# Giving the attention chain of the lead-in an earlier place in the scheduler's order

## The chip, the cores and the metric

The kernel runs on one core of a Trainium2 chip. The metric is the device time of one execution in microseconds (us). The core's engines are TensorE (PE, with its weight loads PEld), VectorE (DVE), ScalarE (ACT), GpSimd (POOL) and SyncE (SP), whose queue starts the DMAs.

## What is computed

Three stages follow each other on 4608 tokens (8 batches of 576) of width 512, all in float32: attention over pooled keys and values, an MoE-like layer with a SoLU and a layer norm, and a SiLU layer.

```python
k_p = k.reshape(B, H, Sp, 8, D).mean(axis=3);  v_p = v.reshape(B, H, Sp, 8, D).mean(axis=3)
scores = (q @ k_p.T) / sqrt(D)                 # B = H = 8, 576 queries, 72 pooled keys
attn = exp(scores - max);  attn = attn / (attn.sum() + 1e-9)
x = attn @ v_p                                  # to (4608, 512)
h = x @ w_in                                    # (4608, 1024)
solu = h * softmax(h);  x = layer_norm(solu) * g_ln @ w_out
h = x @ w2_in;  out = (h * sigmoid(h)) @ w2_out # hidden width 2048
```

The weights arrive as float64 bit patterns (pairs of 32-bit words) and are converted to float32 on the chip.

## The kernel before

Tokens go in 36 tiles of 128. For a tile `t` the words of a small script call the steps: `q` loads queries, `S` (`scores`) multiplies them with the pooled keys and takes the row maximum on DVE and scales it on POOL, `X` (`softmax`) runs 8 exponentials on ACT, a sum and scale on POOL, a reciprocal on DVE and the two products `pb` and `lf` on POOL, `T` (`probs_T`) transposes them on PE and `keep_T` splits the result into a high and a low part with ACT and DVE (`pth`, `ptl`, `ptx`). `A` (`attend_next`) multiplies a segment of 256 or 320 tokens with the pooled values and splits each of four results into `xTh` (ACT) and `xTl` (DVE). `H` (`hidden1`) is the first layer's product, `M`, `E`, `Z` are its maximum (DVE), exponential (ACT) with product (DVE, line 459), and norm (ACT and POOL); `N` transposes the result, `P` (`project1`) is the second product. Names such as S2 or T2 below are the word with its tile, A0 and A1 are segments 0 and 1, and `H0,1,3` is tile 0, half 1 of the hidden width, chunk 3 of the model width.

Beside this run background pieces, called by the word `B`: `prep_k` and `prep_v` load and pool one batch's keys and values, and `load_w1i` and `load_w1o` convert the weights of the first layer, eight pieces each. One piece is a DMA from SP (line 130), an ACT pass (138), three DVE passes (141 `sign`, 142, 145) in `convert`, an ACT copy (155) and a POOL subtraction (156, which writes `w1il` or `w1ol`). A step that needs a piece which no `B` has called calls it itself through `need`. Piece (f, k) of `w1i` is what `H` with half f and chunk k reads.

`SCRIPT` is the lead-in: a hand-written order of words for tiles 0 to 5. After it, `step` runs the script `STEP` once for each later tile. The order on PE is the order of the calls (`manual_schedule` holds PE alone through these stages). ACT, DVE, POOL and SP are ordered by the scheduler: at each point of its own timeline it gives an engine, among the instructions that are ready, the one with the lowest priority number, and that number is the count of instructions emitted so far. So with no other rule a conversion that was emitted before a softmax goes ahead of it when both are ready. Buffers limit it too: the score tile `s` and the hidden tile `h` in PSUM have one buffer each, `g` four, `pth`, `ptl` and `ptx` one, the raw keys and values three.

Emission numbers, counted by the code: S0 26, the first `prep_v` 61, the eight `w1i` pieces 84 to 260, T0 132, T1 142, S2 152, X2 158, T2 178, S3 195, A0 203, X3 232, S4 263 (it calls the four `prep_k` of batch 1 itself, 267 to 283), X4 303, T3 317, M0 332, E0 334, S5 338, Z0 344, T4 352, A1 365, X5 402, T5 468. The lead-in ends at 489, and its first `w1o` piece stands at 444.

```python
elif what == "S":
    scores(*n)
elif what == "X":
    softmax(*n)
```

Of the kernel before, what the change touches and what calls it, by code (L numbers as in the profile page):

```python
# [19 lines left out]
B, H, S, D = 8, 8, 576, 64  # L20
# [42 lines left out]
STEP = "B2 S H0 A B1 H1 M B1 B1 N E P1 X B3 P T B5 p B1 q B2 Z B1 B2"  # L63
TAIL = "H0 A H1 p B2 M N B1 E B2 Z P1 B2 B6 P B2"
RAWS = 3
SCALE = 1.0 / (POOL * math.sqrt(D))
REBIAS = 2.0**-112

# [14 lines left out]
def pooled_attention__solu__silu_kernel(  # L83
# [35 lines left out]
    def gps(name):  # L119
        return ps.tile([P, 512], F32, tag="g", name=name, bufs=4)  # L120
# [48 lines left out]
    def keep_f32(dst, src):  # L169
        w = yield from convert(src, held=True)  # L170
        yield
        nc.sync.dma_start(dst, w)
# [48 lines left out]
    def need(*key):  # L221
        while key not in ready:
            for entry in [e for e in going if e[1] == key]:
                advance(entry)
            for entry in todo:
                if entry[1] == key:
                    todo.remove(entry)
                    advance(entry)
                    break
# [3 lines left out]
    def prep_k(b, p):  # L233
        assert b < 2 or kept["s"] >= (b - 1) * S
        raw = aw.tile([P, SP, POOL], F32, tag="raw", name="raw", bufs=RAWS)
        nc.sync.dma_start(raw, kT[b, :, p])
# [15 lines left out]
    def prep_v(b, p):  # L252
        assert b < 2 or kept["x"] >= (b - 1) * S
        i = b % 2
        raw = aw.tile([P, SP, POOL], F32, tag="raw", name="raw", bufs=RAWS)[:, :D]
        nc.sync.dma_start(raw, vm[b, :, p])
# [13 lines left out]
    def prep_v_rest(b, g):  # L270
        i = b % 2
        raw = aw.tile([P, SP, POOL], F32, tag="raw", name="raw", bufs=RAWS)[0:96, :D]
        nc.sync.dma_start(raw, vl[b, :, g])
# [20 lines left out]
    def load_q(t):  # L294
        q_t[t] = aw.tile([P, NP, P], F32, tag="q", name="q", bufs=3)
        nc.sync.dma_start(q_t[t], qT[t])
# [3 lines left out]
    def scores(t):  # L300
        assert kept["s"] == t * P
        kept["s"] += P
        q = q_t.pop(t)
        sp = ps.tile([P, 2, 512], F32, tag="h" if t == 1 else "s", name="sp")
        done = 0
        while done < P:
            b, s = divmod(t * P + done, S)
            n = min(P - done, S - s)
            need("k", b)
            for p in range(NP):  # L310
                nc.tensor.matmul(  # L311
                    sp[done : done + n, p // 2, (p % 2) * 2 * SP : (p % 2 + 1) * 2 * SP],
                    q[:, p, done : done + n],
                    kbd[b % 2][:, p, :],
                    start=True, stop=True,
                )
            done += n
        sv = sp[:, :, 0 : 4 * SP].rearrange("p a (h k) -> p a h k", k=SP)
        st = aw.tile([P, 2, 2, 4], F32, tag="st", name="st", bufs=3)
        nc.vector.tensor_reduce(st[:, 0], sv, axis=AX, op=ALU.max, negate=True)  # L320
        nc.gpsimd.tensor_scalar(st[:, 0], st[:, 0], SCALE, 0.0, op0=ALU.mult, op1=ALU.add)  # L321
        s_t[t] = st, sv

    def softmax(t):
        st, sv = s_t.pop(t)
        pr = aw.tile([P, 2, 4, SP], F32, tag="pr", name="pr", bufs=2)
        for g in range(2):
            for h in range(4):
                behind["ACT"] = nc.scalar.activation(  # L329
                    pr[:, g, h], sv[:, g, h], AF.Exp, scale=SCALE,  # L330
                    bias=st[:, 0, g, h : h + 1], accum_out=st[:, 1, g, h : h + 1],
                )
        nc.gpsimd.tensor_scalar(
            st[:, 1], st[:, 1], 1e-9, float(POOL), op0=ALU.add, op1=ALU.mult
        )
        nc.vector.reciprocal(st[:, 0], st[:, 1])
        pb = aw.tile([P, 2, 4, 64], F32, tag="pb", name="pb")
        lf = aw.tile([P, 2, 3, 4, 8], F32, tag="lf", name="lf")
        nc.gpsimd.tensor_tensor(
            pb, pr[:, :, :, 0:64],  # L340
            st[:, 0].rearrange("p a (h o) -> p a h o", o=1).to_broadcast([P, 2, 4, 64]),
            op=ALU.mult,
        )
        for g in range(2):
            nc.gpsimd.tensor_tensor(
                lf[:, g],
                pr[:, g, :, 64:SP].rearrange("p (o h) k -> p o h k", o=1).to_broadcast([P, 3, 4, 8]),
                st[:, 0, g].rearrange("p (o h q) -> p o h q", o=1, q=1).to_broadcast([P, 3, 4, 8]),
                op=ALU.mult,
            )  # L350
        p_t[t] = pb, lf

    def seg_of(tok):
        for i, (t0, n, b) in enumerate(SEGS):
            if t0 <= tok < t0 + n:
                return i

    def probs_T(t):
        pb, lf = p_t.pop(t)
        pb = pb.rearrange("p a h k -> p (a h k)")  # L360
        lf = lf.rearrange("p g r h k -> p g (r h k)")
        pm = gps("pm")
        for p in range(NP):
            nc.tensor.transpose(
                pm[:, p * P : (p + 1) * P], pb[:, p * P : (p + 1) * P], ident
            )
        pl = gps("pl")
        for g in range(2):
            nc.tensor.transpose(pl[0:96, g * P : (g + 1) * P], lf[:, g], ident)
        done = 0  # L370
        while done < P:
            i = seg_of(t * P + done)
            m = min(P - done, SEGS[i][0] + SEGS[i][1] - t * P - done)
            if done:
                rest.append((t, pm, pl, i, done, m))
            else:
                keep_T(t, pm, pl, i, done, m)
            done += m
# [3 lines left out]
    def keep_T(t, pm, pl, i, done, m):  # L382
        if i not in pt_t:
            pt_t[i] = (
                aw.tile([P, NP, 320], F32R, tag="pth", name="pth", bufs=1),
                aw.tile([P, NP, 320], F32R, tag="ptl", name="ptl", bufs=1),
                aw.tile([96, 2, 320], F32R, tag="ptx", name="ptx", bufs=1),
            )
        assert kept["p"] == t * P + done
        kept["p"] += m  # L390
        th, tl, tx = pt_t[i]
        o = t * P + done - SEGS[i][0]
        pmv = pm.rearrange("p (a n) -> p a n", n=P)[:, :, done : done + m]
        split(th[:, :, o : o + m], tl[:, :, o : o + m], pmv)
        plv = pl[:, 0 : 2 * P].rearrange("p (a n) -> p a n", n=P)[:, :, done : done + m]
        nc.scalar.activation(tx[:, :, o : o + m], plv[0:96], AF.Copy)
        nc.vector.tensor_tensor(
            tx[64:96, :, o : o + m], plv[64:96], tx[64:96, :, o : o + m].bitcast(F32),
            op=ALU.subtract,
        )  # L400
# [45 lines left out]
    def solu_max(t):  # L446
        assert parts[t, 0] == parts[t, 1] == KC
        hp = h_t[t]
        st = wk.tile([P, 8], F32, tag="ls", name="ls", bufs=3)
        nm, sm, su, sq, a, rs = (st[:, i : i + 1] for i in range(6))  # L450
        nc.vector.tensor_reduce(nm, hp.rearrange("p a n -> p (a n)"), axis=AX, op=ALU.max, negate=True)
        e = wk.tile([P, 2, 512], F32, tag="e", name="e", bufs=2)
        l_t[t] = e, st
# [464 lines left out]
    for n in range(32):  # L918
        what = keep_f32(w2if[n // 4][:, n % 4], w2i[:, n]) if n < 16 else keep_f32(w2of[n % 8][:, (n - 16) // 8], w2o[:, n - 16])
# [19 lines left out]
    def attend_next():  # L939
        nonlocal nseg  # L940
        attend(nseg)
        nseg += 1
        while rest:
            keep_T(*rest.pop(0))
# [7 lines left out]
    def lead_in(script):  # L952
        for word in script.split():
            what, n = word[0], [int(x) for x in word[1:].split(",") if x]
            if what == "q":
                load_q(*n)
            elif what == "S":
                scores(*n)
            elif what == "X":
                softmax(*n)  # L960
            elif what == "T":
                probs_T(*n)
            elif what == "A":
                attend_next()
            elif what == "H":
                hidden1(*n)
            elif what == "M":
                solu_max(*n)
            elif what == "E":
                solu_norm(*n)  # L970
            elif what == "Z":
                solu_scale(*n)
                normed.append(n[0])
            elif what == "N":
                norm_next(*n)
            elif what == "P":
                project1(*chunks.pop(0))
            elif what == "B":
                background(*n)
# [200 lines left out]
```

## Time and profile before

| what | us |
|---|---|
| median of 3 runs | 1404.5 (1402.43 to 1406.67) |
| profiled execution | 1403.74 |
| its span in the trace | 1402.0 |
| PE busy | 1294.8 (92%) |
| DVE busy | 999.4 (71%) |
| ACT busy | 709.1 (51%) |
| POOL busy | 661.5 (47%) |

A span is the time from the first to the last instruction in the trace. Busy time of an engine is the time in which it ran an instruction; an idle engine is given with the one that released it. A view of stretches gives for each stretch the busy time of every engine, PE's granted clock as a share of full speed, and the DMA share.

### The profile page before, as it was taken

The numbers are of one execution on the slowest core, as the hardware profiler recorded it, in microseconds if no ns is written. First come the engines' busy times: TensorE is split into PE (matmuls) and PEld (weight loads), VectorE is DVE, ScalarE is ACT, GpSimd is POOL, SyncE is SP. The second block draws the span as 40 slices with busy tenths as digits, with TensorE's granted clock in tenths as the row PEclk, the third lists the DMA queues.
The fourth block names the chain that finished last, engine by engine and source line by source line (L and its number), as shares of the span: only waits on it lengthen the run. The fifth ranks groups of instructions, "written<-read, shape, count | busy, mean of one in ns | idle before, by whom it ended". The sixth has DMA issues, their size and how long they took to land.

```text
span 1402.0 us, 23904 instructions
## 1 busy us (share of the span) xinstructions
PE 1294.8 (92%) x8712; PEld 1227.4 (88%) x8712; DVE 999.4 (71%) x1438; ACT 709.1 (51%) x1772; POOL 661.5 (47%) x829
## 2 busy tenths in 40 slices
PE   2589899999999999889998999999979999999998
PEld 2469789988989899789888988999979999999998
DVE  6896566766766565445787889888547788877785
ACT  4684555565555555343554555554433444434442
POOL 5674344444444433444555666777323333433332
PEclk7899999999999999999999999999989999999999
DMA  7655244543434211122566678665776344444431
GB/s 227 207 159 164 80 130 143 156 139 114 140 99 128 91 61 61 61 76 94 194 243 250 245 266 307 238 237 195 294 271 255 128 151 151 151 129 143 134 95 74
DMA packets 100550, 227.01 MB, mean 162 GB/s; under 512 B 8272, under 2 KB 29776, under 8 KB 98896
## 3 DMA queue, kind: packets, MB, share of 16 engines
q1 hardware_dynamic: 96400, 210.80, 45.1%
q10 hardware_dynamic: 4032, 14.68, 2.8%
q8 instruction: 69, 1.13, 0.3%
q14 instruction: 49, 0.40, 0.1%
HBM read 141.56 MB, written 83.89 MB: 161 GB/s over the span
## 4 chain that ended last, share of the span: by engine, by line
PE 49%; DVE 7%; issue 5%; DMA 4%; ACT 3%; POOL 2%; SPq 0%; ACTq 0%; DVEq 0%; POOLq 0%
PE op L853 24%; PE m L707 12%; PE xp L510 6%; PE hp L440 5%; DVE gt L717 2%; DVE wr L529 1%; PE tp L490 1%; DMA w2r<-w2if 1%; DVE t L529 1%; DVE u L717 1%; ACT gt L677 1%; DMA x2r<-x2d 1%; PE sp L311 1%; DMA w2o<-wod 1%; DVE w2r L529 1%
## 5 line engine op out<-in xcount | busy, mean ns | idle before, releaser
L707 PE MATMUL m<-t,w2s 128*128 128x384 f32 x2016 | 367.2, 340 | 23.9 <-DVE gt L717 11.8
L707 PEld LDWEIGHTS m<-t,w2s 128*128 128x128 f32 x2016 | 352.4, 190 | 38.3 <-DVE gt L717 14.6
L853 PE MATMUL op<-w2o,gt 128*128 128x256 f32 x3024 | 368.0, 284 | 8.5 <-ACT gt L830 7.9
L853 PEld LDWEIGHTS op<-w2o,gt 128*128 128x128 f32 x3024 | 366.0, 193 | 10.5 <-ACT gt L830 8.8
L529 DVE TENSOR_TENSOR gt<-gr,gt 128x512 fp32r<-128x512 f32 x180 | 164.7, 949 | 67.4 <-ACT gt L830 67.4
L830 ACT ACTIVATE gt<-gr 128x512 fp32r<-128x512 f32 x180 | 103.2, 623 | 151.4 <-DVE gr L529 132.5
L717 POOL TENSOR_TENSOR gt<-u,m 128x384 f32<-128x384 f32 x96 | 114.5, 1203 | 134.3 <-ACT m L727 91.8
L510 PE MATMUL xp<-lnh,w1oh 128*128 128x256 f32 x576 | 168.1, 292 | 0.5 <-ACT lnh L123 0.2
L510 PE MATMUL xp<-lnl,w1oh 128*128 128x256 f32 x576 | 163.9, 285 | 1.1 <-DVE lnl L124 1.1
L510 PE MATMUL xp<-lnh,w1ol 128*128 128x256 f32 x576 | 163.8, 284 | 0.0
L440 PE MATMUL hp<-w1ih,xTh 128*128 128x512 f32 x288 | 119.0, 413 | 8.9 <-DVE e L459 8.9
L736 ACT ACTIVATE gt<-gt 128x768 f32<-128x768 f32 x48 | 40.7, 847 | 157.2 <-DVE gt L717 157.2
L811 POOL TENSOR_TENSOR s<-gr 128x512 f32<-128x512 f32 x36 | 58.3, 1618 | 127.1 <-DVE gt L529 74.2
L329 ACT ACTIVATE pr<-sp,st 128x72 f32<-128x72 f32 x288 | 88.3, 330 | 56.8 <-POOL st L321 56.7
L440 PE MATMUL hp<-w1il,xTh 128*128 128x512 f32 x288 | 115.5, 401 | 0.6 <-POOL w1il L156 0.6
L440 PE MATMUL hp<-w1ih,xTl 128*128 128x512 f32 x288 | 115.7, 402 | 0.3 <-DVE xTl L124 0.3
L510 PEld LDWEIGHTS xp<-lnh,w1oh 128*128 128x128 f32 x576 | 111.4, 193 | 1.7 <-DVE lnl L124 0.7
L510 PEld LDWEIGHTS xp<-lnl,w1oh 128*128 128x128 f32 x576 | 111.6, 194 | 1.4 <-DVE lnl L124 1.3
L510 PEld LDWEIGHTS xp<-lnh,w1ol 128*128 128x128 f32 x576 | 111.3, 193 | 0.0
L529 DVE TENSOR_TENSOR t<-tt,t 128x768 fp32r<-128x768 f32 x48 | 64.8, 1354 | 14.1 <-ACT t L640 14.0
L440 PEld LDWEIGHTS hp<-w1ih,xTh 128*128 128x128 f32 x288 | 56.3, 196 | 21.1 <-issue 9.2
L830 ACT ACTIVATE gt<-s 128x512 fp32r<-128x512 f32 x72 | 42.1, 621 | 62.6 <-POOL s L529 56.6
(129 smaller groups left out, 2352.4 us busy)
## 6 DMA issues: line engine op xcount, KB each, us to landing
gd<-gt SPq DMA_DIRECT2D x48, 768.0 KB, 4.5
gr<-gd SPq DMA_DIRECT2D x48, 512.0 KB, 6.2
x2r<-x2d SPq DMA_DIRECT2D x12, 1536.0 KB, 7.6
wod<-wo SPq DMA_DIRECT2D x56, 256.0 KB, 2.7
gr<-gd SPq DMA_DIRECT2D x48, 256.0 KB, 5.4
q<-qT SPq DMA_DIRECT2D x36, 256.0 KB, 3.2
raw<-kT SPq DMA_DIRECT2D x32, 288.0 KB, 3.5
x2d<-xo SPq DMA_DIRECT2D x18, 512.0 KB, 3.4
```

The costliest lines, as they stand in the source:

```text
L311: nc.tensor.matmul(sp[done : done + n, p // 2, (p % 2) * 2 * SP : (p % 2 + 1) * 2 * SP], q[:, p, done : done + n], kbd[b % 2][:, p, :], st ...
L329: behind["ACT"] = nc.scalar.activation(pr[:, g, h], sv[:, g, h], AF.Exp, scale=SCALE, bias=st[:, 0, g, h : h + 1], accum_out=st[:, 1, g, h ...
L440: nc.tensor.matmul(hp[:, f], l, r, start=(n == 1 and m == 0), stop=(n == KC and m == 2))
L490: nc.tensor.transpose(tp[:, k * P : (k + 1) * P], e[:, f, k * P : (k + 1) * P], ident)
L510: nc.tensor.matmul(xp[:, :GW], l, r, start=(k == 0 and m == 0), stop=(k == FC1 - 1 and m == 2))
L529: eng.tensor_tensor(dst, a, b, op=ALU.subtract)
L707: nc.tensor.matmul(to, wt[:, a, o : o + P], tk[:, b, k], start=(k == 0 and m == 0), stop=(k == 1 and m == 2),)
L717: eng.tensor_tensor(dst, a, b, op=ALU.add)
L736: nc.scalar.activation(gt[:, 0], gt[:, 0], AF.Silu)
L811: nc.gpsimd.tensor_tensor(s1, a21, a22, op=ALU.add)
L830: nc.scalar.activation(ring[n][:, 0], src, AF.Copy)
L853: nc.tensor.matmul(op[:, 256 * h : 256 * h + 256], t[:, l, i, ts], w[:, r], start=(s == i == h == m == 0), stop=(s == NSET - 1 and i == h ...
```

## The change

The words `S`, `X`, `T` and `A` of the lead-in are called inside a block that lowers the priority number of all that is emitted in it by 100. On leaving the block the count goes on as before. Nothing is added to or removed from the work; the later steps and PE's order stand as they were.

```diff
+AHEAD = 100
@@ lead_in
-            elif what == "S":
-                scores(*n)
-            elif what == "X":
-                softmax(*n)
-            elif what == "T":
-                probs_T(*n)
-            elif what == "A":
-                attend_next()
+            elif what in "SXTA":
+                with tc.high_priority(offset=AHEAD):
+                    {"S": scores, "X": softmax, "T": probs_T, "A": lambda x: attend_next()}[what](*n)
```

## Rows read from the trace of the kernel before

**Rows 1.** The page: busy time, share of the span, instructions.
```profile
PE 1294.8 (92%) x8712; PEld 1227.4 (88%) x8712; DVE 999.4 (71%) x1438; ACT 709.1 (51%) x1772; POOL 661.5 (47%) x829
```

**Rows 2.** Stretches: length, busy time by engine, granted clock, DMA share, GB/s.
```profile
60.40:66.20 5.80, 2.17 (x14) 1.67 (x14) 4.40 (x8) 5.14 (x17) 3.73 (x9) 1.00 0.65 226
...
68.40:71.70 3.30, 0.01 (x1) 0.01 (x1) 1.26 (x2) 2.45 (x9) 1.75 (x5) 1.00 0.61 171
71.70:75.10 3.40, 3.40 (x11) 3.15 (x12) 3.23 (x7) 3.11 (x13) 2.81 (x5) 0.52 0.16 19
...
95.00:106.00 11.00, 9.34 (x51) 7.85 (x50) 10.91 (x23) 10.29 (x36) 9.57 (x14) 1.00 0.68 196
...
200.00:300.00 100.00, 94.92 (x629) 86.82 (x628) 68.56 (x115) 56.90 (x189) 45.18 (x96) 0.97 0.49 148
```

**Rows 3.** PE's waits, 0 to 110 us: total, times, longest.
```profile
PE pm L364 <- POOL pb L339: 23.1, 5, 12.9
...
PE av L415 <- DVE xTl L124: 5.7, 2, 3.3
PE hp L440 <- DVE e L459: 5.3, 3, 2.6
```

**Rows 4.** Timeline, S2 to T2: start, length, engine, line, what [idle before].
```profile
26.43 2.13 PE L311 MATMUL sp<-kbd,q 128*128 128x144 f32 x8
...
29.23 3.76 DVE L141 TENSOR_SCALAR sign<-raw 128x512 int32<-128x512 int32 x1
...
30.22 2.48 POOL L156 TENSOR_TENSOR w1il<-w,w1ih 128x512 fp32r<-128x512 f32 x2
...
34.19 0.76 DVE L320 TENSOR_REDUCE st<-sp 128x8 f32<-128x576 f32 x1
...
41.44 1.12 PE L364 MATMUL pm<-ident,pb 128*128 128x128 f32 x4 [12.88 <-POOL pb L339]
```

**Rows 5.** Timeline, the last piece of `w1i` and its reader H0,1,3.
```profile
52.19 0.68 DVE L145 SCALAR_TENSOR_TENSOR w<-raw,w 128x512 int32<-128x512 int32 x1
...
54.93 1.28 POOL L156 TENSOR_TENSOR w1il<-w,w1ih 128x512 fp32r<-128x512 f32 x1
...
56.26 0.50 PE L440 MATMUL hp<-w1il,xTh 128*128 128x512 f32 x1 [0.63 <-POOL w1il L156]
```

**Rows 6.** Timeline, the end of tile 0's H, and A1.
```profile
61.71 0.20 DVE L336 RECIPROCAL st<-st 128x8 f32<-128x8 f32 x1 [1.41 <-POOL st L333]
...
66.25 0.47 PE L440 MATMUL hp<-w1ih,xTh 128*128 128x512 f32 x1 [1.82 <-DVE e L459]
...
70.69 0.42 ACT L123 ACTIVATE xTh<-av 128x320 fp32r<-128x320 f32 x1
...
71.15 1.12 DVE L124 TENSOR_TENSOR xTl<-av,xTh 128x320 fp32r<-128x320 f32 x2 [1.98 <-ACT xTh L123]
...
71.69 0.51 PE L415 MATMUL av<-pth,vbh 128*128 128x320 f32 x1 [3.33 <-DVE xTl L124]
```

**Rows 7.** Timeline, the start: key loads, and DVE's first conversion.
```profile
2.11 1.38 SPq L236 DMA_DIRECT2D raw<-kT  x3
...
14.98 0.43 DVE L141 TENSOR_SCALAR sign<-raw 128x512 int32<-128x512 int32 x1 [1.10 <-DMA raw<-w1i]
```

**Rows 8.** Timeline, the last `w1ol` and the first project1 (first, last needed).
```profile
104.43 1.31 POOL L156 TENSOR_TENSOR w1ol<-w,w1oh 128x512 fp32r<-128x512 f32 x1 [0.46 <-ACT w1oh L155]
...
106.17 0.36 PE L510 MATMUL xp<-lnh,w1oh 128*128 128x256 f32 x1
...
109.00 0.28 PE L510 MATMUL xp<-lnh,w1ol 128*128 128x256 f32 x1
```

**Rows 9.** Groups by line: count, busy us, mean ns, idle before; 28 to 106 us, exponentials whole span.
```profile
L141 DVE TENSOR_SCALAR sign<-raw 128x512 int32<-128x512 int32 x13 | 10.1, 778 | 0.0
...
L339 POOL TENSOR_TENSOR pb<-pr,st 128x512 f32<-128x512 f32 x5 | 5.5, 1097 | 3.8 <-DVE st L336 2.0 <-PE hp L440 1.4 <-PE av L415 0.4
...
L329 ACT ACTIVATE pr<-sp,st 128x72 f32<-128x72 f32 x288 | 88.3, 330 | 56.8 <-POOL st L321 56.7
```

## The prediction

> **What bounds the kernel now.** I read the busy times first: PE works 92% of the span [rows 1], so PE is the bound as a whole, and between 200 and 300 us it is busy 94.92 of 100 us [rows 2]. Such a middle passes on what happens before it about one to one: if PE gets through the lead-in 1 us sooner, the end comes about 1 us sooner. The change touches the lead-in alone, so next comes the list of PE's waits up to 110 us. The largest is T waiting for the softmax product `pb`: 23.1 us in 5 waits, one of 12.9 [rows 3]. Then come A waiting for `xTl` (5.7 in 2) and H waiting for tile 0's and later tiles' product of line 459, which frees the one hidden buffer (5.3 in 3).
>
> Then the timeline behind the longest wait. S2's matmuls end at 26.43 + 2.13 = 28.56, but DVE takes their maximum at 34.19, because it has conversions in front of it in its queue, among them a `sign` pass of 3.76 us, and T2 starts only at 41.44 [rows 4]. That is the loss which the change aims at. But PE runs in a fixed order, so the question is what it meets after T2. It meets H0,1,3, which needs the last of the eight `w1i` pieces: its last DVE pass is at 52.19, its POOL pass ends at 54.93 + 1.28 = 56.21, and the matmul that waits for it starts at 56.26 [rows 5]. PE was there only 0.63 us too early. So **two chains of nearly equal length meet at 56.26**: the attention chain, and the conversion chain, and the change shortens one at the cost of the other.
>
> The third thing to see is DVE. In 95 to 106 us it is busy 10.91 of 11 us [rows 2], and it is the queue through which both chains go. What it leaves idle between 60 and 75 us is 5.80 - 4.40 = 1.40 and 3.30 - 1.26 = 2.04 [rows 2].
>
> **The change part by part.** The number of each instruction of S, X, T, A falls by 100, so S2 (152) stands at 52 and A0 (203) at 103, ahead of nearly all the `w1i` pieces (84 to 260). Nothing is added. What moves with it: every ACT, DVE and POOL instruction of these words, and the DMAs that they issue themselves on SP, which are the four key loads of batch 0 (in S0) and of batch 1 (in S4). SP's queue and POOL's queue are passed as DVE's is.
>
> *Start.* S0's key loads are issued at 2.11, behind the first queries and the gains [rows 7]. They go first now, so 2.11 us sooner at the very most. It reaches the conversions only in part, since DVE's first one waits for its own DMA at 14.98 [rows 7], and the bytes ahead of that one are the same. I take a quarter, -0.5, with bounds of -2.1 and +0.5 (the same the other way, if the queries now come late).
>
> *T2.* The maximum of S2 can run when its matmuls are done, at about 29.2 (28.56 and one short DVE instruction) instead of 34.19. From the maximum to T2 it was 41.44 - 34.19 = 7.25 us and needs no more now, so T2 comes at some 36.4, 5.0 us sooner. On PE this is worth **nothing by itself**: the cover is gone that hid the conversions, and H0,1,3 waits at 56 instead of T2 at 41. PE reaches it at about 51 (56.26 - 0.63 - 5.0).
>
> *The gate, the last `w1i` piece.* The DVE work in front of it is the same as before except for what now overtakes it: S4's maximum (0.76, as the row of S2's) and one reciprocal (0.20) [rows 4, 6], +0.96. Against that, S2's maximum (0.76) moves out of the conversions' way into time in which they wait for their ACT passes. Sum +0.2, so 56.5. Its bounds: -3.3, if the `sign` pass of 3.76 us drops to the 0.43 of the undisturbed one [rows 4, 7]; and +8.0, worked out under the slower rival.
>
> That long `sign` pass lies under GpSimd work without a gap (the two `w1il` passes from 30.22 last to 32.70, and it ends at 32.99) [rows 4]. The Trainium skill ("SBUF — State Buffer", "Who interferes with whom") says that the two engines share a pair of ports and that whichever instruction starts first holds it to its end while the other blocks. By that rule the pass would have waited for one GpSimd instruction, about 1.24 us here, not 3.3; the trace agrees that it waits but not on how long, and the measurement decides. By the rule's price the slower rival below would end some 2 us lower.
>
> *Clock.* After a wait of 3.33 us at A1 PE's granted clock was 0.52 for 3.40 us, the lower of its two levels (1.2 GHz), and full after that [rows 2, 6]. PE will now stand idle for some 5 to 6 us ahead of H0,1,3, longer than that wait. Matmuls at half the clock lose half the stretch: 0.48 x 3.40 = 1.6 us, which come on the path. +1.6, bounds 0 (if the conversions come no later than PE) and +1.6.
>
> *From H0 to H1.* DVE stood idle 1.41 us ahead of a reciprocal of tile 4 that had been queued in front of M0 [rows 6]: tile 4's softmax was late. Now it is done while PE waits for the gate, and M0 can start when H0 ends. -1.3 (0.1 for the reciprocal's place), bounds -1.8 (the whole of the wait at 66.25 [rows 6]) and 0.
>
> *A1.* PE waits 3.33 us for `xTl`, DVE 1.98 for `xTh`, because ACT ran tile 0's norm first and `xTh` only at 70.69 [rows 6]. A1 (365) now stands at 265, ahead of the norm (344). The split itself cannot go: 0.42 on ACT and 0.5 on DVE [rows 6], about 0.9. -2.4, and the clock that fell behind this wait stays up, -1.6. Bounds -4.0 and 0: the scheduler places what is ready, and the norm can be ready first.
>
> The sum on PE is -0.5 + 0.2 + 1.6 - 1.3 - 2.4 - 1.6 = **-4.0**. The other limit is DVE: from 75 us on it has no time free, and its work does not shrink, so it can be early only by the idle time that goes: 1.41 of the reciprocal, 1.98 - 0.5 of A1, and the 0.5 of the start, together **-3.4**. The later of the two counts, -3.4; the difference comes back as longer waits for line 459. What is late next is the last `w1ol`: it ends at 105.74 and the matmul that reads it starts at 109.00 [rows 8], 3.3 us of room, so with PE 3.4 us early it must move by 0.1 only, and DVE's own 3.4 give that.
>
> The profiled execution took 1403.74, 1.74 above its span of 1402.0; the median of the runs is 0.76 above it. 1402.0 - 3.4 + 1.74 + 0.76 = **1401.1**.
>
> **The rivals.**
> *Faster: the conversions speed up as well.* The 13 `sign` passes between 28 and 106 us take 10.1 us, mean 0.778, against 0.43 undisturbed [rows 7, 9]: 4.5 us are lost to overlap with GpSimd. If the new mix, with conversions and POOL's chain work in other places, avoids the one long stall (-3.3), gate and DVE both come sooner, -6.7 in all, 1397.8. For it: that stall is the largest single loss on DVE. Against it: POOL's work is the same, and DVE meets it somewhere.
> *Absorbed, or not done.* The scheduler orders by its own timeline; where on it the chain is ready late, or the norm first, the order at M0 and A1 stays, and what is gained at T2 ends at the gate. Then 0, 1404.5. T2 alone cannot show the gain.
> *Slower: the last `w1i` piece falls behind the chain on three engines.* X4 (303) stands at 203 now, ahead of that piece's instructions (251 to 260). Its place is ACT, where eight exponentials of 0.33 (2.6) can stand ahead of the piece's pass, then POOL, where a `pb` of 1.1 can [rows 9], then DVE with the 0.96 above, and one more stall of 3.3: together +8.0 at the gate. The gains behind it, with the clock, are -0.5 + 1.6 - 1.3 - 2.4 - 1.6 = -4.2, so it decides from a gate more than 4.2 us late. At 8.0 the kernel is 3.8 slower, 1408.3. For it: the two chains meet within 0.63 us today, so each microsecond counts. Against it: most of these would have to come in series.
>
> **How the numbers follow.** Forecast (1401.1) 0.42, faster (1397.8) 0.28, absorbed (1404.5) 0.15, slower (1408.3) 0.15. About 0.3%, 4.2 us, is what a measurement of this kernel can tell from no change. The unknown terms (start, gate, A1) spread each case by some 2.5 us: of the forecast case a third lies below 1400.3, of the faster one nine tenths, of the slower one some four tenths above 1408.7, and a little of every case lies outside by the order of later steps, which shifts as well. Faster 0.41, same 0.46, slower 0.13. The range reaches from 1394.5 (the faster case less its spread) to 1408.5 (the slower one).
>
> **What would show it.** T2 at 35 to 37 us and the `pb` waits of PE cut from 23.1 to some 15; a new wait of PE at H0,1,3 for `w1il`, of 4 to 8 us, ending at 55 to 58; a low clock behind it; H1's first matmul at about 65.5 to 66.5; A1 without the 3.3 us wait; the first project1 at about 102.8 instead of 106.17 [rows 8]; then the same shift to the end. The prediction is wrong if the gate moves by more than 3 us either way, if A1's wait stays, or if PE's gain at 75 us is gone at 106.

## The result, and the profile after

The changed kernel takes 1418.85 us (median of 6 runs, 1410.96 to 1421.6), against 1404.8 of the kernel before (6 runs). The ratio is 1.0092, 95% interval 1.0068 to 1.0116: it is **slower by 0.9%**, where 1401.1 was forecast. The profiled execution took 1415.32, its span 1413.5, which is 11.5 us more than before. It is 3.5 us faster than the median, so the 11.5 us taken apart below stand for 14.05 by the medians. The lines quoted here stand one further down than before (440 is L441, 459 is L460, 339 is L340), and in some of the experiments two.

The page's busy times first (they answer to [rows 1]):

```profile
PE 1298.7 (92%) x8712; PEld 1230.0 (87%) x8712; DVE 998.8 (71%) x1438; ACT 710.2 (50%) x1772; POOL 659.3 (47%) x829
```

The instructions are the same in number and nearly the same in time; PE has 3.9 us more, and the other 7.6 of the 11.5 us are idle time on it. The waits of PE from 0 to 120 us (line, releaser, total, times, longest; [rows 3] are those of before):

```profile
PE hp L441 <- DVE e L460: 15.1, 3, 8.0
PE hp L441 <- ACT w1ih L156: 14.2, 2, 13.7
PE pm L365 <- POOL pb L340: 12.7, 3, 6.3
...
PE av L416 <- DVE xTl L125: 3.9, 3, 1.6
PE hp L441 <- POOL w1il L157: 2.4, 2, 1.9
```

The waits for `pb` fell from 23.1 to 12.7, as the change means to. In their place stand 14.2 us for the first-layer weights `w1ih` in two waits, one of 13.7, and the wait for `e` has grown from 5.3 to 15.1. PE's timeline in the changed kernel shows where they are (start, length, line, what, idle before and its releaser):

```profile
29.79 1.12 PE L365 MATMUL pm<-ident,pb 128*128 128x128 f32 x4 [5.70 <-POOL pb L340]
...
46.15 3.07 PE L312 MATMUL sp<-kbd,q 128*64 128x144 f32 x16
62.91 0.80 PE L441 MATMUL hp<-w1ih,xTh 128*128 128x512 f32 x1 [13.69 <-ACT w1ih L156]
64.26 0.79 PE L441 MATMUL hp<-w1il,xTh 128*128 128x512 f32 x1 [0.55 <-POOL w1il L157]
...
70.63 1.14 PE L312 MATMUL sp<-kbd,q 128*128 128x144 f32 x8
...
80.39 0.76 PE L441 MATMUL hp<-w1ih,xTh 128*128 128x512 f32 x1 [7.97 <-DVE e L460]
...
85.79 0.64 PE L416 MATMUL av<-pth,vbh 128*128 128x320 f32 x1 [1.64 <-DVE xTl L125]
...
101.55 0.77 PE L441 MATMUL hp<-w1ih,xTh 128*128 128x512 f32 x1 [5.12 <-DVE e L460]
...
123.11 0.36 PE L511 MATMUL xp<-lnh,w1oh 128*128 128x256 f32 x1
```

These are T2, S4, H0,1,3 (its first and its `w1il` matmul), S5, the first matmuls of H1, of A1's third result and of H2, and the first project1. In the kernel before S5 stands at 61.45 and H2 at 84.61; the others are in [rows 4 to 6, 8].

| event on PE | before | after | shift | change of the shift |
|---|---|---|---|---|
| T2 | 41.44 | 29.79 | -11.65 | |
| H0,1,3, `w1il` (the gate) | 56.26 | 64.26 | +8.00 | +8.00 |
| S5 | 61.45 | 70.63 | +9.18 | +1.18 |
| H1 | 66.25 | 80.39 | +14.14 | +4.96 |
| A1, third result | 71.69 | 85.79 | +14.10 | -0.04 |
| H2 | 84.61 | 101.55 | +16.94 | +2.84 |
| first project1 | 106.17 | 123.11 | +16.94 | 0.00 |
| end of the span | 1402.0 | 1413.5 | +11.5 | -5.44 |

So there are **two losses**: 8.0 us at the gate, the last `w1i` piece, and 5.0 between S5 and H1 (tile 0's maximum M0 and exponential E0), with two smaller ones (1.2 and 2.8); 5.4 come back later. Of these, 3.6 lie between 120 and 150 us, where PE of the kernel before still has one wait of 3.6 and PE of the changed kernel has none. The view of stretches (length, busy PE, PEld, DVE, ACT, POOL, clock, DMA share, GB/s), first of the kernel before, then of the changed one:

```profile
120.00:150.00 30.00, 26.40 (x169) 23.87 (x168) 16.39 (x28) 10.10 (x37) 10.79 (x26) 0.89 0.57 171
```

```profile
120.00:150.00 30.00, 30.00 (x222) 28.43 (x221) 14.36 (x28) 15.50 (x58) 11.02 (x29) 1.00 0.28 84
```

**The first loss: the gate.** The place to look is DVE up to the end of the third pass of the last `w1i` piece, at 52.19 + 0.68 = 52.87 before [rows 5] and at 62.19 after. DVE's groups in these stretches (line, what, count, busy us, mean ns, idle before them), before:

```profile
L142 DVE SCALAR_TENSOR_TENSOR w<-w,sign 128x512 int32<-128x512 int32 x8 | 6.1, 768 | 1.2 <-ACT w L138 1.2
L241 DVE TENSOR_REDUCE kp<-raw 128x72 f32<-128x576 f32 x8 | 5.9, 746 | 7.9 <-DMA raw<-kT 7.8
L261 DVE TENSOR_REDUCE vp<-raw 128x64 f32<-128x512 f32 x5 | 3.4, 671 | 1.2 <-DMA raw<-vm 1.2
L320 DVE TENSOR_REDUCE st<-sp 128x8 f32<-128x576 f32 x4 | 3.0, 750 | 0.0
...
L278 DVE TENSOR_REDUCE vlp<-raw 96x64 f32<-96x512 f32 x2 | 1.3, 650 | 0.0
```

and after:

```profile
L143 DVE SCALAR_TENSOR_TENSOR w<-w,sign 128x512 int32<-128x512 int32 x8 | 8.4, 1054 | 0.6 <-ACT w L139 0.6
L242 DVE TENSOR_REDUCE kp<-raw 128x72 f32<-128x576 f32 x10 | 7.3, 747 | 5.6 <-DMA raw<-kT 5.5
...
L262 DVE TENSOR_REDUCE vp<-raw 128x64 f32<-128x512 f32 x8 | 5.4, 680 | 3.2 <-DMA raw<-vm 3.2
L321 DVE TENSOR_REDUCE st<-sp 128x8 f32<-128x576 f32 x5 | 3.8, 754 | 4.7 <-PE sp L312 4.7
L279 DVE TENSOR_REDUCE vlp<-raw 96x64 f32<-96x512 f32 x4 | 2.6, 662 | 0.0
```

Up to the end of that pass the groups sum to 48.5 us instead of 42.1 (neighbouring instructions overlap a little; counted once, DVE is busy 45.05 instead of 39.35), and DVE is idle 17.2 instead of 13.5. Of the 6.4 us in the sums 5.5 are work that has come forward: three `vp` and two `vlp` passes of batch 1's values (3.3), two `kp` passes of batch 2's keys (1.4) and S4's maximum (0.8). Only the last of these is in a leading word. The loads of batch 1's values are issued on SP from 26.80 on instead of 39.84, right behind batch 1's four key loads (17.11 to 26.14 instead of 21.21 to 39.26), with which they share the three raw buffers: what follows a led step through its buffers comes forward too. Of the idle time 4.7 stand in front of score maxima, most of it in front of S4's. The three engines at that moment, from their timelines in the changed kernel:

```profile
49.26 0.76 DVE L321 TENSOR_REDUCE st<-sp 128x8 f32<-128x576 f32 x1 [3.85 <-PE sp L312]
...
50.44 0.32 ACT L330 ACTIVATE pr<-sp,st 128x72 f32<-128x72 f32 x1 [3.92 <-POOL st L322]
...
50.10 0.30 POOL L322 TENSOR_SCALAR st<-st 128x8 f32<-128x8 f32 x1 [4.04 <-DVE st L321]
```

DVE, ACT and POOL have S4's softmax at the head of their queues and stand still for 4 us until PE has run S4's matmuls, and PE hadn't come to S4 sooner because a chunk of H0 ahead of it in PE's order had itself waited for a `w1i` piece (1.86 us, up to 43.72). Conversions queued behind could have run: two pieces had their ACT pass behind them by 43.14 and 44.38, but their first DVE passes stand at 49.93 and 53.14, and a third had its `w1ih` by 46.07, but its `w1il` stands at 50.48. In numbers (the columns as above):

```profile
44.80:49.30 4.50, 4.42 (x20) 3.27 (x18) 0.65 (x3) 1.46 (x3) 0.73 (x1) 0.54 0.64 184
49.30:62.20 12.90, 0.00 (x0) 0.00 (x0) 12.78 (x16) 5.19 (x21) 11.10 (x14) 0.62 0.53 171
```

First PE is the only full engine, then DVE is full, POOL nearly (11.10), and PE does nothing for 12.9 us.

**The second loss: M0 and E0.** H1 needs the one hidden buffer, which tile 0's maximum, exponential and product free. ACT's and DVE's timelines, first of the kernel before, then of the changed one:

```profile
63.36 1.14 ACT L458 ACTIVATE e<-hp,ls 128x1024 f32<-128x1024 f32 x1
...
67.28 0.32 ACT L329 ACTIVATE pr<-sp,st 128x72 f32<-128x72 f32 x1 [1.74 <-POOL st L321]
```

```profile
61.83 1.17 DVE L451 TENSOR_REDUCE ls<-hp 128x1 f32<-128x1024 f32 x1
...
64.87 1.23 DVE L459 SCALAR_TENSOR_TENSOR e<-hp,e 128x1024 f32<-128x1024 f32 x1
```

```profile
74.94 0.32 ACT L330 ACTIVATE pr<-sp,st 128x72 f32<-128x72 f32 x1 [0.68 <-POOL st L322]
...
77.02 0.35 ACT L330 ACTIVATE pr<-sp,st 128x72 f32<-128x72 f32 x1
77.31 1.15 ACT L459 ACTIVATE e<-hp,ls 128x1024 f32<-128x1024 f32 x1
```

```profile
73.62 1.21 DVE L452 TENSOR_REDUCE ls<-hp 128x1 f32<-128x1024 f32 x1
...
79.01 1.22 DVE L460 SCALAR_TENSOR_TENSOR e<-hp,e 128x1024 f32<-128x1024 f32 x1
```

Tile 0's maximum ends at 74.83, but its exponential starts at 77.31, behind all eight exponentials of tile 5. In the kernel before it stood at 63.36, ahead of those eight (67.28 to 72.21). X5 (402) has been taken past E0 (334). M0 (332) is late as well: it starts 2.84 us after H0's last matmul ends (70.78), instead of 1.44 after (60.39), behind a conversion's third pass, T3's two splits and S5's maximum on DVE. From H0's last matmul to H1 it takes 9.6 us instead of 5.9, of which M0's start accounts for 1.4 and E0's for 2.1; the rest of the 5.0 is mainly the wait of 1.06 that the kernel before had ahead of S5 and the changed one hasn't.

### The profile page after: what moved, and what is told of

It reads as the page before. It is cut to its first block, busy times and chain, and to the rows that moved or that the text cites. A ratio compares the mean times of both kernels' runs of the same rounds, so it can differ in the third digit from the quotient of the medians.

```text
span 1413.5 us, 23902 instructions
## 1 busy us (share of the span) xinstructions
PE 1298.7 (92%) x8712; PEld 1230.0 (87%) x8712; DVE 998.8 (71%) x1438; ACT 710.2 (50%) x1772; POOL 659.3 (47%) x829
## 4 chain that ended last, share of the span: by engine, by line
PE 43%; DVE 9%; issue 6%; DMA 5%; ACT 4%; POOL 2%; SPq 0%; ACTq 0%; DVEq 0%; POOLq 0%
PE op L854 24%; PE m L708 7%; PE xp L511 6%; PE hp L441 5%; DVE gt L718 2%; DMA w2r<-w2if 1%; DVE u L718 1%; DMA gd<-gt 1%; DVE wr L530 1%; DMA gr<-gd 1%; DVE wo L530 1%; DVE t L530 1%; PE tp L491 1%; ACT gt L678 1%; DMA x2r<-x2d 1%
## 5 line engine op out<-in xcount | busy, mean ns | idle before, releaser
L441 PE MATMUL hp<-w1ih,xTh 128*128 128x512 f32 x288 | 120.7, 419 | 31.4 <-DVE e L460 17.2
L441 PE MATMUL hp<-w1il,xTh 128*128 128x512 f32 x288 | 117.2, 407 | 2.4 <-POOL w1il L157 2.4
L441 PE MATMUL hp<-w1ih,xTl 128*128 128x512 f32 x288 | 117.0, 406 | 0.0
L441 PEld LDWEIGHTS hp<-w1ih,xTh 128*128 128x128 f32 x288 | 57.0, 198 | 44.5 <-issue 18.0
L530 DVE TENSOR_TENSOR t<-tt,t 128x768 fp32r<-128x768 f32 x48 | 63.4, 1324 | 13.7 <-ACT t L641 13.6
```

Source lines behind the costliest of these rows:

```text
L441: nc.tensor.matmul(hp[:, f], l, r, start=(n == 1 and m == 0), stop=(n == KC and m == 2))
L530: eng.tensor_tensor(dst, a, b, op=ALU.subtract)
```

## The experiments

Where words are named, only these lead, by this edit:

```diff
+FIRSTS = "S2 X2 T2".split()
-                with tc.high_priority(offset=AHEAD):
+                with tc.high_priority(offset=AHEAD) if word in FIRSTS else ExitStack():
```

Ratios are to the kernel before, with 95% intervals.

**The first half of the words** (S0 X0 S1 X1 T0 T1 S2 X2 T2 S3 A0 X3).

> The lead of 100 is kept for the words from S0 to X3 alone; S4, X4, T3, S5, T4, A1, X5 and T5 keep their plain numbers. Theory Q (head of the queue): the loss is made where S4's maximum, its scale and tile 4's exponentials stand ahead of the last three w1i pieces on DVE, POOL and ACT while PE, in its fixed order, is not at S4 yet. Then most of the loss goes: at most 1409 us, DVE without the idle 3.9 us ahead of S4's maximum, the last w1il start at 55 to 58 us. Theory P (first pieces): the loss is made at the first w1i pieces, which come 7.8 us late (their third DVE pass at 27.4 instead of 19.1) behind the softmax of tiles 0 and 1, and never catch up. Then at least 1414 us, the last w1il at 61 us or later.

1.0082 (1.0054 to 1.011). Nearly the whole loss, and so a miss for the theory that S4's words make it. The gate is at 63.17, though S4 doesn't lead and DVE's last `w1i` pass is over at 54.82 + 1.20 = 56.02. What holds it is POOL (its timeline in this run):

```profile
56.15 1.70 POOL L270 TENSOR_TENSOR vbl<-vp,vbh 64x256 fp32r<-64x256 f32 x2
57.93 0.78 POOL L285 TENSOR_TENSOR vlh<-vlp,vlh 32x128 fp32r<-32x128 f32 x1
58.79 1.37 POOL L341 TENSOR_TENSOR pb<-pr,st 128x512 f32<-128x512 f32 x1
60.12 1.32 POOL L347 TENSOR_TENSOR lf<-pr,st 128x96 f32<-128x96 f32 x2
61.41 1.71 POOL L158 TENSOR_TENSOR w1il<-w,w1ih 128x512 fp32r<-128x512 f32 x1
```

The last `w1il` stands behind batch 1's values and tile 4's `pb` and `lf`. So the gate is held by a queue in this run too, but by another one.

**The second half** (S4 X4 T3 S5 T4 A1 X5 T5).

> The lead of 100 is kept for S4, X4, T3, S5, T4, A1, X5 and T5 alone; the words before keep their plain numbers. Theory Q: most of the loss is here, 1410 us or more. Theory P: the first pieces come as before (third DVE pass at 19 us), so the time is that of before within 3 us, 1402 to 1408.

1.0071 (1.0047 to 1.0096). The gate is at 58.52 (the last `w1il` ends at 57.99, 1.8 later than before), S5 at 62.91; then H1 waits 9.77 for `e` and comes at 75.67, 9.4 later than before. M0 starts 3.2 after H0's last matmul ends, and on ACT E0 starts at 71.84, 4.9 after M0 ends, behind tile 5's eight exponentials (69.46 to 71.55). This half has the second loss with little of the first.

**The changed kernel with a count that goes on.** On leaving the block the priority count falls back to what it was at its start (it doesn't go on as before, as the section on the change has it), so that later words have smaller numbers than in the kernel before. This run takes it forward again:

```diff
+                at_word = tc.cur_priority
                 with tc.high_priority(offset=AHEAD):
                     ...
+                    emitted = tc.cur_priority - at_word + AHEAD
+                tc.cur_priority = at_word + emitted
```

> All words lead by 100, but the count of emitted instructions goes on past each block instead of returning to its value at the block's entry, so the conversions behind a block do not slide up to it as well and the four key loads of batch 1 lead by less over the w1i pieces. Theory Q: S4 (163 on this count) is still ahead of the last pieces (251 on), so there is still a loss, 1409 to 1416 us. Theory P: the first pieces are overtaken just the same, 1414 to 1420 us. A third theory, that the returned count makes the loss: 1405 us or less.

1.0085 (1.0056 to 1.0114): the loss stays, with the gate at 60.08 and 6.69 of waiting ahead of H1. So the returned count isn't needed for the loss, though about half of the gate's delay goes with it; that this doesn't show in the time wasn't followed up.

**The changed kernel with S4 called earlier**, right behind X3 and so ahead of H0,0,3.

```diff
-X3 H0,0,3 B1,2 B1,-7 B3,-7 H0,0,2 S4 B1,9
+X3 S4 H0,0,3 B1,2 B1,-7 B3,-7 H0,0,2 B1,9
```

> The changed kernel with the word S4 moved in the script to the place right behind X3, so that on PE it stands ahead of H0,0,3 and H0,0,2 and no longer waits for the conversions that these wait for. Theory Q: the idle 3.9 us of DVE ahead of S4's maximum go, and with them some 4 us or more of the loss, 1409 to 1415 us. Theory P: 1416 to 1421 us, as the changed kernel.

1.0083 (1.0056 to 1.0109). A miss for the theory that S4 at the head of the queues is the loss: DVE's idle time there falls to 1.60 and its last `w1i` pass is over at 55.93 instead of 62.19, but the gate goes only from 64.26 to 62.82. POOL holds it: it runs the last two `w1il` passes from 59.67 to 62.77, behind batch 1's values (`vbl`, `vlh`, `vls`). With one obstacle away the other holds the gate.

**The second half, with M0 and E0 leading as well.**

```diff
+                with tc.high_priority(offset=AHEAD) if n[0] == 0 else ExitStack():
                     solu_max(*n)
```

(the same round `solu_norm`)

> The lead of 100 for S4, X4, T3, S5, T4, A1, X5 and T5 as in the run e_back, and for M0 and E0 too, so that tile 5's softmax no longer overtakes tile 0's exponential. Theory E (the overtaken E0): of the loss of e_back (H1's first matmul at 75.7 us instead of 66.3, PE waiting 9.8 us for the product of tile 0) some 8 us come from tile 0's exponential, which stands behind tile 5's maximum, scale and eight exponentials. Then H1's first matmul is back at 66 to 69 us and the time at 1403 to 1408. Rival C (conversions): the words cost time by holding up the conversions, wherever E0 stands: 1411 us or more.

0.9997 (0.9982 to 1.0012): the loss of the second half is gone. M0 starts 0.45 after H0's last matmul and E0 0.20 after M0 (65.52, ahead of tile 5's exponentials at 70.54). PE's timeline of this run has H1 at 68.56 instead of 75.67:

```profile
68.56 0.62 PE L442 MATMUL hp<-w1ih,xTh 128*128 128x512 f32 x1 [2.48 <-DVE e L461]
```

So the second loss is **shown** to be M0 and E0 passed over. Both lead in this run, so it doesn't part them; in the second half's trace E0 waited longer (4.9 against 3.2).

**Parts of the first half**: S0 X0 S1 X1 T0 T1; then S2 X2 T2; then S3 A0 X3.

> The lead of 100 for S0, X0, S1, X1, T0 and T1 alone, the words that overtake the first w1i pieces. Theory P (first pieces): the late first piece is what makes the last one late; its third DVE pass comes at 25 us or later instead of 19, the last w1il starts at 59 us or later, and the time is 1411 us or more. Rival S (S2 to A0): the first words cost little, since DVE has idle time there; the last w1il starts at 54 to 57 us, the time is 1402 to 1408.

1.0044 (1.0029 to 1.006). T2 at 35.59, gate 0.6 late (56.86), H1 3.0 late. The first `w1i` piece's third DVE pass comes 5.9 later than before (24.90 instead of 19.05), so a late first piece doesn't hold the gate by itself.

> The lead of 100 for S2, X2 and T2 alone, the words behind PE's longest wait of before (12.9 us). Theory P: the first pieces come as before, T2 comes some 5 us sooner, the gate at H0,1,3 moves by 3 us at most: 1401 to 1408 us. Rival S: these words hold up the conversions: 1409 us or more, the last w1il at 59 us or later.

1.0019 (1.0006 to 1.0033). The cleanest test of the prediction's first step. PE's timeline of this run:

```profile
36.09 1.12 PE L366 MATMUL pm<-ident,pb 128*128 128x128 f32 x4 [7.61 <-POOL pb L341]
...
55.00 0.50 PE L442 MATMUL hp<-w1ih,xTh 128*128 128x512 f32 x1 [2.20 <-ACT w1ih L157]
56.34 0.80 PE L442 MATMUL hp<-w1il,xTh 128*128 128x512 f32 x1 [0.84 <-POOL w1il L158]
...
68.89 0.62 PE L442 MATMUL hp<-w1ih,xTh 128*128 128x512 f32 x1 [4.04 <-DVE e L461]
```

T2 is 5.35 us earlier, the gate 0.08 later, and nothing is gained (0.19% is lost); from the gate to S5 it then takes 6.72 us instead of 5.19, since the matmuls there are 0.43 apart and not 0.23.

> The lead of 100 for S3, A0 and X3 alone. Theory P: no loss, 1401 to 1408 us. Rival S: X3's eight exponentials on ACT and its products on POOL, ahead of the third and fourth w1i pieces, make the gate late: 1409 us or more.

1.0036 (1.0025 to 1.0047). A miss: here the conversions are *earlier* (the last `w1il` ends at 53.70) and H1 comes at 65.41, 0.84 before its time, and still it is slower: A1 waits 3.98, H3 3.57, and the first project1 is at 112.45, 6.3 late. The three parts sum to 0.99%, the whole half has 0.82 (0.54 to 1.1).

**The changed kernel with M0 and E0 leading.**

> The change as it stands, and M0 and E0 (tile 0's maximum and exponential with the product of line 460) lowered by 100 as well, so that tile 5's softmax no longer goes ahead of E0. Theory of two causes (the late first conversions hold H0,1,3; the overtaken E0 holds H1): H0,1,3 stays at 62 to 64 us, H1's wait for e falls from 7.97 to 2 to 3 us, H1 comes at 74 to 76 instead of 80.39, the first project1 at 116 to 119, and the time is 1409 to 1413, that is, between the kernel before and the change. Rival, E0 alone: back to 1404. Rival, gate alone: the busy stretch behind takes back what E0 gains, 1416 to 1419.

1.0049 (1.0034 to 1.0064). About half of the loss is back, as two causes need. The gate stays at 64.05, H1 comes at 76.37 instead of 80.39, H2 at 94.82 instead of 101.55. 7.8 us are lost at the gate, 10.1 at H1, 9.3 at the first project1 and 8.5 in the span.

**The reverse: the chain keeps its place and the `w1i` pieces lead.**

```diff
     def load_w1i(f, k):
         fs = slice(512 * f, 512 * f + 512)
-        yield from load_split(w1ih[:, k, fs], w1il[:, k, fs], w1i[:, k, fs])
+        piece = load_split(w1ih[:, k, fs], w1il[:, k, fs], w1i[:, k, fs])
+        for _ in range(3):
+            with tc.high_priority(offset=AHEAD):
+                if next(piece, "end") == "end":
+                    return
+            yield
```

> The reverse: S, X, T and A keep their place and each w1i piece is lowered by 100. If the conversion chain is what the lead-in ends on (it set the gate in the kernel before, the attention chain having 0.63 us to spare), the last w1il ends by 50 to 54 instead of 56.21, but the keys and the softmax wait behind it, T2 comes at 44 to 50 instead of 41.44, and the gate passes to the attention chain: H0,1,3 at 56 to 62, time 1405 to 1411. Rival, slack in the attention chain: T2 as before, H0,1,3 at 53 to 55, time 1400 to 1402.

1.0014 (1.0002 to 1.0027). The last `w1il` ends at 40.01, 16.2 us sooner, and now the chain is the gate: T2 waits 8.01 and comes at 44.63, H0,1,3 at 57.67 instead of 55.13 (inside the expected range), S5 at 65.74 instead of 61.45. The last `w1il` came far sooner than the 50 to 54 expected. In this direction too the chain that is passed over becomes the gate.

**M0 and E0 with S3 A0 X3.**

> S3, A0 and X3 lowered by 100 as in the run that had the last w1il pass start at 52.43 and H1 at 65.41 and yet lost 4.8 us, and M0 and E0 lowered too. If that loss is E0's product held up on the way to H1 and H2: H1 at 64 to 65, the first project1 at 105 to 108, time 1402 to 1405. Rival, the loss comes from the w1o conversions or later words pushed back: H1 at 64 to 65 but the first project1 at 111 to 113 again, time 1408 to 1410.

1.0052 (1.0037 to 1.0067), no better than without M0 and E0. The loss has gone to a later softmax: tile 6's exponentials run between the `w1o` passes on ACT (84.99 to 92.0), its reciprocal stands at 95.46 on DVE behind tile 2's maximum and product, and PE waits at T6:

```profile
98.72 1.12 PE L366 MATMUL pm<-ident,pb 128*128 128x128 f32 x4 [8.44 <-POOL pb L341]
```

In the kernel before that T waits 0.35.

**A lead of 20 instead of 100.**

> The change with a lead of 20 instead of 100. The first pieces still stand behind the keys, values and scores of tiles 0 and 1. If the loss grows with what is overtaken: T2 at 33 to 38, H0,1,3 at 57 to 60, H1 at 69 to 74, time 1407 to 1413. Rival, the returned count alone gives the chain its lead whatever the number: as the change, T2 at 30, H0,1,3 at 62 to 64, time 1416 to 1419.

1.0051 (1.0032 to 1.0071). T2 at 34.23; the last `w1il` ends at 57.77, and PE reads it at 57.83, 1.6 late; but H1 comes at 75.00 after a wait of 8.92. Most of this is DVE's queue ahead of M0 (its timeline):

```profile
65.11 3.35 DVE L142 TENSOR_SCALAR sign<-raw 128x512 int32<-128x512 int32 x1
68.38 0.68 DVE L125 TENSOR_TENSOR ptl<-pm,pth 128x512 fp32r<-128x512 f32 x1
69.09 0.42 DVE L398 TENSOR_TENSOR ptx<-pl,ptx 32x256 fp32r<-32x256 f32 x1
69.54 0.76 DVE L321 TENSOR_REDUCE st<-sp 128x8 f32<-128x576 f32 x1
70.22 1.22 DVE L452 TENSOR_REDUCE ls<-hp 128x1 f32<-128x1024 f32 x1
```

H0's matmuls are over when S5 begins at 64.29, but M0 waits behind a stalled `sign` pass, two splits of transposed probabilities and tile 5's maximum. So the smaller lead nearly spares the gate and still loses at M0. None of these twelve kernels is faster than the kernel before.

**The gate over all runs.** The reverse apart, the end of the last `w1il` goes with the number of batch 1's six value passes (`vp`, `vlp`) that DVE runs before the last `w1i` piece's third pass: with one, 53.70 to 56.29 (the kernel before, S2 X2 T2, and S3 A0 X3 with and without M0 and E0); with two or three, 56.81 to 57.99 (S0 to T1, the second half with and without M0 and E0, the lead of 20); with four, 60.03 (the count that goes on); with all six, 62.77 to 64.20 (the changed kernel, it with M0 and E0, the first half, S4 called earlier). This points at the values on DVE and POOL, but no run held them back alone, so it isn't shown that they are the cause.

## Why the prediction was wrong

**T2.** It came 11.65 us earlier, not 5.0, since the words before it lead too; with S2, X2 and T2 alone it comes at 36.09, where 36.4 was worked out. That this is worth nothing by itself was right: the same run is 0.19% slower.

**The start.** -0.5 was forecast. DVE's first conversion pass came 0.74 later (15.72 instead of 14.98), and the first piece's third pass 8.3 later (27.35 instead of 19.05), behind the softmax of tiles 0 and 1. The run with S0 to T1 shows that this alone moves the gate by 0.6 only.

**The gate: the step that failed first.** The prediction named it as the meeting point of two chains and gave +0.2 with a bound of +8.0; it is +8.00. The wrong sentence is that the DVE work in front of the last piece is the same but for S4's maximum and one reciprocal. Five passes of batch 1's values and two of batch 2's keys went in front as well, 4.7 us, and S4 brought 4 us in which DVE, ACT and POOL stood idle behind it, which no term had. These are what the trace shows in front; they don't add up as separate causes, since without most of S4's idle time the gate gained only 1.4. The slower rival had the size of the delay by luck: it was made up of tile 4's exponentials and `pb` and one more stall, without the values and the idle time. Its `pb` on POOL ahead of the piece is seen in the run with the first half; in the changed kernel itself the last piece is late on DVE.

**The clock.** +1.6 was forecast. From the gate to S5 it took 6.37 instead of 5.19, +1.18, of which the kernel before had spent 1.06 waiting at S5 that the changed one doesn't wait: the lower clock cost 2.2, and 1.1 of it took the place of that wait. The mechanism was right. The granted clock behind the wait (the columns as above):

```profile
62.90:69.10 6.20, 5.64 (x12) 3.98 (x13) 6.13 (x10) 3.57 (x6) 3.56 (x4) 0.50 0.79 252
80.30:84.00 3.70, 3.61 (x11) 3.09 (x11) 3.70 (x6) 2.05 (x5) 3.21 (x7) 0.50 0.76 214
```

0.50 is the lower of the two levels, 1.2 GHz. The second row is a miss: the sum counted on the full clock around A1 (-1.6), but behind the new wait of 7.97 ahead of H1 it is 0.50 there too, where the kernel before had 1.00 (66.25 to 68.40).

**From S5 to H1: the second step that failed.** -1.3 was forecast, +4.96 measured. The prediction saw that tile 4's softmax would be early and counted this as a gain for M0. It didn't ask what the led words pass: M0 on DVE and E0 on ACT aren't among them. M0 came 1.4 later behind H0 instead of 1.3 sooner, and E0 2.1 later behind M0. The run with M0 and E0 leading beside the second half settles this.

**A1.** Its wait fell from 3.33 to 1.64, 1.7 of the 2.4 forecast; the gain is nil on the path: from H1 to A1's third result it takes 5.40 us instead of 5.44, since PE needs 3.76 at the clock of 0.50 for the matmuls ahead of the wait, where it needed 2.11.

**H2.** +2.84 had no term. It waits 5.12 for tile 1's product, where 2.61 were before; why wasn't followed up, but with M0 and E0 leading this wait is 3.32.

**What passes on.** The prediction took a loss before 106 us to reach the end one to one. In the changed kernel 16.94 at the first project1 became 11.5, in part because PE of the kernel before has a wait of 3.6 after 120 us. Over the runs the two are only loosely tied: 9.3 and 8.5 with M0 and E0 leading, 11.4 and 14.7 for the first half, 4.7 and 0.3 for the second half with M0 and E0, 4.9 and 6.1 for the reverse. Each is one execution, and executions of the kernel before alone lie up to 11 us apart (1399.96 to 1411.05), so one-to-one is neither shown nor refuted.

**The rivals.** The slower one named the right place and the right +8.0 and gave 1408.3, since it kept gains of 4.2 behind the gate; there it lost another 3.5 instead (11.5 - 8.0; by the medians 6). The faster one, that the long `sign` stall goes, has this against it: `sign` passes did get shorter (6.0 us for nine instead of 7.3 for eight), but the second pass got longer by as much and more (8.4 for eight instead of 6.1).

**What stays open.** What holds the last `w1i` piece is read from the traces and not taken away in a run. Why leading S3, A0 and X3 loses 0.36% although the gate and H1 come earlier was seen (A1, H3, the later `w1o`) but not taken apart; and leading M0 and E0 beside them moved the loss to T6 instead of removing it. That small leads each cost something fits a kernel in which DVE's queue is full through the lead-in, but no run shows that as a rule.

## What to carry to other kernels

Before giving a chain priority, list for each engine what it is taken past and who waits for *that*: here the weight pieces of the next matmul, and the maximum and exponential that free a single buffer. Count what the led step calls on its own and what follows it through shared buffers, and remember that an instruction at the head of a queue that waits for its operand stops everything behind it, as S4's maximum did for 3.85 us here. Where the two chains meet within 0.63 us of each other, each direction of priority lost here (0.92% and 0.14%); whether less work or less idle time in the shared queue would gain, no run tried.

## What was unexpected in the hardware

A DVE pass can wait for several GpSimd instructions in a row. The last `w1i` piece's third pass in the changed kernel (59.51, 2.68 us instead of 0.68) ends at 62.19, 0.55 after the end of three `vls` instructions and a `w1il` that run on POOL without a gap from 58.91 to 61.64; the `sign` pass of 3.35 us shown above ends at 68.46, 0.3 after two `w1ol` that end at 68.17, and the one of 3.76 [rows 4] has the same form. All three begin while `vls` runs. Not every pass does this: the second pass of the last piece (58.09, 1.39 us) ends at 59.48, 0.55 after a `w1il` that ends at 58.93, although `vls` follows that `w1il` without a gap. What parts the two cases isn't shown. The first of these waits lies in the gate itself, where that pass takes 2.0 us more than undisturbed. The Trainium skill ("SBUF — State Buffer", "Who interferes with whom") lets the wait end with the one instruction that holds the ports. The pass from 58.09 agrees with that; the three long ones don't, as the kernel before already showed for one of them, and there the measurement decides.
